# Attention and a squared-ReLU feed-forward on one core: the first product of the last 1024 tokens as seven block products, w_out's products in another order, attention's values two visits behind its scores

## The chip, the core and the metric

The kernel runs on one core of a Trainium2 chip. The metric is device time in microseconds. The time before is 602.68 us, the median of three runs (601.35 to 603.2).

## The reference, cut to what matters

Four sequences of 768 tokens with 8 heads of 64 go through a local attention with block summaries, and its output goes through a feed-forward of 512 -> 2048 -> 512:

```python
k_sum = k.reshape(B, H, nb, block, D).max(axis=3)        # block = 32
v_sum = v.reshape(B, H, nb, block, D).mean(axis=3)
scores_l = scale * q @ k.T, kept where abs(i - j) < 16
scores_s = scale * q @ k_sum.T + log(block)
a = softmax(concat(scores_l, scores_s))
attn = a @ concat(v, v_sum)
x = attn.transpose(0, 2, 1, 3).reshape(B * S, H * D)     # 3072 x 512
h = x @ w_in                                             # 512 x 2048
g = maximum(h, 0) ** 2
return g @ w_out                                         # 2048 x 512
```

## The kernel before, in words

Every operand of the feed-forward is split into a high and a low part (`xh`, `xl`; `gh`, `gl`; two parts of each weight tile), and each product is the sum of three (high x high, low x high, high x low). The 3072 tokens form six units of 512 tokens. A unit is eight groups of 64 tokens, and attention is done group by group, in visits of TensorE (`visit`, L809): one visit does the scores of two new groups (L597) and the products with the values of two older ones (L803), before at the distance of one visit. Between them lies a softmax on VectorE and ScalarE, a transpose of the probabilities on VectorE (L776, tile `a`), and a turn through DRAM: four stores to `turn` (L787) and one fetch (L793). The result of the values is split into `xh` and `xl` (L867, L870), a ring of 16 groups.

Units 0 and 1 (`ffn`, L955) are done plainly: for each of the 16 slices f of w_in, 12 matmuls of 128x512 give `h` (L979), ScalarE makes the ReLU and its square, and 12 matmuls with w_out's slice add up the output (L1003). In unit 0 the weights are also loaded and split.

The other 2048 tokens are two halves s = 0 and 1 of two units each. Their first product (`first_product`, L1183) is plain: 16 slices of 12 matmuls per unit (L1203). For their second product g is seen as 2 x 2 blocks (two slices f, two units), w_out likewise, and a scheme of seven block products replaces eight (`products`, L1238). A product j runs over the eight slice pairs p, with six matmuls of 128x512 for each p (L1316), so 56 steps of six for each s. Five operands of w_out's side are sums of blocks, made once by GpSimd (`combine`, L1062, with L1070 and L1085) and kept in DRAM; each step loads its 256 KB with a DMA (L1286) into a ring of eight places. On the side of g, three of the seven operands are sums of blocks made in place by VectorE (L1295), two more come out of the second unit's squares (L1232). For each step ScalarE makes the high part `gh` (L1300) and VectorE the low part `gl` (L1305); each of the two has three buffers. TensorE does four matmuls with `gh`, then two with `gl`. VectorE takes the finished products from PSUM (L1263).

The order on each engine is worked out before the program is recorded: every task has an engine, a cost, a key (when it is wanted) and the tasks and buffers that it needs, and a planner (`Plan.order`, L136) places them by key. On the chip each engine takes its instructions in that order, and waits by semaphores for the data alone. GpSimd also moves the block maxima of the keys (L610), which the next visit's scores need. All DMAs are issued from SyncE's queue.

Of the kernel before, what the change touches and what calls it, by code (L numbers as in the profile page):

```python
# [20 lines left out]
P = 128  # L21
# [15 lines left out]
NV = 3  # L37
# [12 lines left out]
FV_LEAD, FV1_LEAD = 2.0, 17.0  # L50
# [54 lines left out]

class Task:
# [6 lines left out]
class Plan:  # L113
# [13 lines left out]
    def add(self, name, engine, cost, emit, key, after=(), take=(), use=(), size=0, begin=0.0, behind=None, late=0.0):  # L127
        t = Task(name, engine, cost, emit, key, [a for a in after if a is not None], list(take), list(use), size, begin)
        t.behind, t.late = behind, late
        t.index = len(self.tasks)  # L130
        self.tasks.append(t)
        for b in t.take + t.use:
            b.users.append(t)
        return t

    def order(self):  # L136
# [29 lines left out]
        while events:  # L166
# [11 lines left out]
            for e, tasks in ready.items():  # L178
# [3 lines left out]
                t = next((t for t in tasks if t.begin <= now + 1e-9 and (t.behind is None or hasattr(t.behind, "start")) and can(t)), None)  # L182
# [23 lines left out]
def attention_then_relu2_ffn(  # L206
# [95 lines left out]
    FIRST_STEP = 3.2, 3.1, 2.8, 2.9  # L302
    PRODUCT_STEP = 1.55, 1.5, 1.4, 1.4
    A0, A1, B0, B1 = 12.0, 2.0, 21.0, 2.2
    HALF_AT = 25.0, 32.0
    SECOND = 0.0
    steps = [SLOW, STEP, *FIRST_STEP]
    unit_at, products_at, at = [], [], T0
    for u in range(NU):
        unit_at.append(at)  # L310
        at += NF * steps[u]
        if u >= PLAIN:
            products_at.append(at)
            at += (SOON, PRODUCTS - SOON)[(u - PLAIN) % 2] * NQ * PRODUCT_STEP[u - PLAIN]
    at_item = {(u, f): unit_at[u] + f * steps[u] for u, f in items}

    def wanted(g):
# [4 lines left out]
        lo, hi = unit_at[u - 1] + SECOND * (u == 1), unit_at[u] - LEAD * STEP  # L322
        if u >= NU - 2:
            ends = unit_at[NU - 3] - LEAD * STEP, unit_at[NU - 1] - LEAD * STEP
            mid = min(sum(ends) / 2, unit_at[NU - 2] - LEAD * STEP)
            lo, hi = (ends[0], mid) if u == NU - 2 else (mid, ends[1])
# [131 lines left out]
    def batch_v(b):  # L458
        key = wanted(b * NW - 1) - (FV_LEAD if b > 1 else FV1_LEAD) if b else -60
        out_ps = h_buf(f"vps{b}")  # L460
# [14 lines left out]
        for i in range(0, S // P, 2):  # L475
            if b == 1:
                x, xs = later_v[i], later_v[i : i + 2]
            elif b:
                x = buf("t", 3, (P, 2 * DM), F32, f"fv{b}_{i}")
# [4 lines left out]
            for k in range(2):  # L484
                new = not k and (b > 1 or i % 4 == 0)
# [3 lines left out]
                    key + (0.1 if b else 1) * (i + k) - 4 * (not b), behind=None if new else t, take=[x] * bool(new), use=[x] * (not new),  # L489
# [157 lines left out]
    def softmax(g, by_pe=False):  # L647
# [124 lines left out]
        else:  # L772


            def turn():
                nc.vector.transpose(  # L776
                    out=a.tile.rearrange("p (j n r) -> p j n r", j=NSQ, n=NPAIR),
# [4 lines left out]
            t_T[g] = add(f"T{g}", "DVE", 0.63, turn, due - 9, [t_n], take=[a], use=[pr])  # L782
            d = buf("turn", 4, (NSQ, SQ, NSQ, NPAIR * SQ), F32, f"turn{g}", dr)

            def store():
                for i in range(NSQ):
                    nc.sync.dma_start(  # L787
                        out=d.tile[:, :, i, :].rearrange("j c e -> c j e"),
                        in_=a.tile[i * SQ : (i + 1) * SQ].rearrange("c (j e) -> c j e", j=NSQ),
# [5 lines left out]
            t_w = add(f"TW{g}", "SP", 1.75, store, due - 8.5, [t_T[g]], take=[d], use=[a], size=4 * P * DM)  # L795
            t_A[g] = add(f"TR{g}", "SP", 0.35, fetch, due - 8, [t_w], use=[a, d], size=4 * P * DM)
# [11 lines left out]

    def visit(both, then=(), block_sums=None):  # L809

        n, g = len(both), both[-1]
        due = wanted(g)
        x_ps = h_buf(f"x{g}") if n == 2 else x_buf(f"x{g}")
# [9 lines left out]
        means_too = []  # L823
        take = [x_ps]
# [5 lines left out]
        if then:  # L830
# [4 lines left out]
            deps += keys_of(then[0], range(NPAIR)) + [t_QL[then[1]], window(then[1])] + [t_T[g] for g in both]  # L835
# [4 lines left out]
        def products():  # L840
# [8 lines left out]
            f"V{both[-1]}", "PE", 0.54 * n + 0.11 * (n == 1) + 0.49 * len(then) + 1.4 * bool(block_sums), products, due, deps,  # L849
            take=take + [s] * bool(s), use=use,  # L850
# [3 lines left out]
        for f in means_too:  # L854
            f()
        for g in then:
            t_S[g] = [t_v]
        cols = slice(both[0] % RING * TQ, (both[-1] % RING + 1) * TQ)
# [196 lines left out]
    scr_i = [dr.tile([P, 2 * DM], F32, name=f"scr_i{i}", tag=f"scr_i{i}") for i in range(NQ)]  # L1055


    ORDER = (0, 0), (0, 1), (1, 0), (1, 1), (1, 2), (0, 2), (1, 3)
# [3 lines left out]
    def combine(p):  # L1062

        due = unit_at[0] + 75 + 13.5 * p
        ws = [w_parts[1, 2 * p + k] for k in range(2)]
        raw = buf("t", 3, (P, 2 * DM), F32, f"cr{p}")
        sums = buf("t", 3, (P, 2 * DM), F32, f"cs{p}")
# [6 lines left out]
        def part(k, i):  # L1074
            return raw.tile[:, k * DM + i * HALF : k * DM + (i + 1) * HALF]
# [4 lines left out]
        def add_up():  # L1080
            for i, a, b, op in (
                (2, part(0, 1), part(1, 1), ALU.add), (0, of(2), part(0, 0), ALU.subtract),
                (1, part(0, 0), part(0, 1), ALU.subtract), (3, part(1, 0), of(0), ALU.subtract),
# [9 lines left out]
        def store():  # L1093
            for w, x in enumerate((raw, sums)):
                nc.sync.dma_start(
                    out=scr_s[p].rearrange("c p w x -> p c w x")[:, :, w], in_=x.tile.rearrange("p (c x) -> p c x", c=4)
                )
# [8 lines left out]
        for k in range(2):  # L1106
            t1.append(add(
                f"RC{p}_{k}", "POOL", 1.3, lambda k=k: whole(k), due + 1.3 * k, t_W[1, 2 * p + k],
                take=[raw, sums] * (not k), use=[raw] * k + ws[k], begin=due, behind=t1[0] if k else None,
            ))  # L1110
# [367 lines left out]
```

## Time and profile before

| | |
|---|---|
| median of three runs | 602.68 us |
| time of the profiled execution | 600.91 us |
| its span | 598.8 us |
| TensorE matmul busy | 581.8 us, 97% |
| VectorE busy | 394.1 us, 66% |
| ScalarE busy | 340.9 us, 57% |
| GpSimd busy | 67.3 us, 11% |
| granted TensorE clock | 0.999 |
| DMA traffic | 134.7 MB on the queue of the kernel |

PE is TensorE's matmuls, PEld its weight loads, DVE VectorE, ACT ScalarE, POOL GpSimd and SPq the queue of SyncE, from which DMAs are issued. In a row of a timeline stand the start, the duration, the engine, the line of the kernel, the operation, what it writes and reads, the size, how many, and in brackets how long the engine stood idle before it and who ended that. Lines are those of the kernel before.

### The profile page before, as it was taken

Reading aid. Unit: us, or ns where it says so; the run is one execution under the profiler, and the core shown is the slowest. Engines: PE = TensorE matmul, PEld = TensorE weight load, DVE = VectorE, ACT = ScalarE, POOL = GpSimd, SP = SyncE. Lnnn points to the kernel's source line nnn. Section 1 sums busy time; section 2 is a strip of 40 time slices with the busy share of each in tenths; the row PEclk is TensorE's granted clock in tenths of the full one; section 3 lists DMA queues with packets and bytes.
Section 4 is the critical chain, followed back from the end, with each engine's and each line's share of the span. In section 5 each row is a group of like instructions: output and inputs, shape, how many; then the busy total and the mean of one; then the engine's idle time right before and its main releaser. Section 6 shows DMA issues by size and latency. Waiting matters only on the chain.

```text
span 598.8 us, 11522 instructions
## 1 busy us (share of the span) xinstructions
PE 581.8 (97%) x4132; PEld 476.1 (80%) x4132; DVE 394.1 (66%) x692; ACT 340.9 (57%) x844; POOL 67.3 (11%) x117
## 2 busy tenths in 40 slices
PE   8889999979999999999999999999999999999996
PEld 6778888868888888888888787788888878888885
DVE  5999997767646815336855859897553643349763
ACT  2999885757736635446745656645453643455442
POOL 4300004333555200000000000000000000000000
PEclk9999999999999999999999999999999999999999
DMA  8999966859987885736856956889823762126772
GB/s 308 314 399 334 366 204 208 277 171 364 366 276 260 255 278 155 260 107 185 255 181 188 306 180 192 273 277 295 264 76 97 234 197 97 36 85 207 188 234 96
DMA packets 94428, 135.43 MB, mean 226 GB/s; under 512 B 9676, under 2 KB 50636, under 8 KB 94372
## 3 DMA queue, kind: packets, MB, share of 16 engines
q1 hardware_dynamic: 94372, 134.70, 69.6%
q8 instruction: 33, 0.54, 0.3%
q14 instruction: 23, 0.19, 0.1%
HBM read 98.22 MB, written 35.65 MB: 224 GB/s over the span
## 4 chain that ended last, share of the span: by engine, by line
PE 77%; DMA 8%; DVE 6%; ACT 6%; SPq 2%; issue 1%; DVEq 0%; ACTq 0%
PE h L1203 28%; PE o L1316 23%; PE o L1003 10%; PE h L979 9%; DMA raw<-wW 4%; PE x L803 3%; PE att L597 3%; ACT p L728 2%; DVE w L933 1%; DMA v<-vS 1%; DVE t L925 1%; DMA fv_lent<-vS 1%; DMA a<-turn 1%; DMA qvpa_lent<-qW 1%; ACT w L930 1%
## 5 line engine op out<-in xcount | busy, mean ns | idle before, releaser
L1203 PE MATMUL h<-xh,w 128*128 128x512 f32 x448 | 138.8, 391 | 0.5 <-ACT r L1213 0.5
L1316 PE MATMUL o<-gh,w 128*128 128x512 f32 x448 | 121.0, 391 | 0.4 <-ACT gh L1300 0.4
L1300 ACT CAST gh<-g 128x512 fp32r<-128x512 f32 x112 | 68.9, 620 | 53.3 <-DVE gl L1305 25.8
L1203 PEld LDWEIGHTS h<-xh,w 128*128 128x128 f32 x448 | 83.6, 188 | 18.7 <-ACT r L1213 1.3
L1316 PEld LDWEIGHTS o<-gh,w 128*128 128x128 f32 x448 | 83.5, 188 | 18.4 <-ACT gh L1300 0.9
L1305 DVE TENSOR_TENSOR gl<-g,gh 128x512 fp32r<-128x512 f32 x112 | 76.0, 687 | 28.4 <-ACT gh L1300 28.3
L1203 PE MATMUL h<-xl,w 128*128 128x512 f32 x224 | 87.2, 389 | 0.0
L1213 ACT ACTIVATE r<-h 128x512 f32<-128x512 f32 x64 | 38.0, 596 | 86.3 <-PE h L1203 73.0
L979 PE MATMUL h<-xh,w 128*128 128x512 f32 x240 | 74.1, 390 | 0.0
L728 ACT ACTIVATE p<-p,nm 128x118 f32<-128x118 f32 x160 | 61.1, 388 | 16.6 <-DVE nm L692 16.6
L1316 PE MATMUL o<-gl,w 128*128 128x512 f32 x224 | 69.4, 390 | 1.1 <-DVE gl L1305 1.1
L1003 PE MATMUL o<-w,gh 128*128 128x512 f32 x240 | 61.6, 393 | 1.9 <-ACT gh L990 1.9
L1003 PEld LDWEIGHTS o<-w,gh 128*128 128x128 f32 x240 | 44.5, 188 | 11.7 <-ACT gh L990 2.3
L979 PEld LDWEIGHTS h<-xh,w 128*128 128x128 f32 x240 | 44.9, 188 | 9.4
L1316 PEld LDWEIGHTS o<-gl,w 128*128 128x128 f32 x224 | 41.9, 188 | 10.6 <-DVE gl L1305 2.0
L1203 PEld LDWEIGHTS h<-xl,w 128*128 128x128 f32 x224 | 42.0, 188 | 8.8
L979 PE MATMUL h<-xl,w 128*128 128x512 f32 x120 | 46.7, 389 | 0.0
L993 DVE TENSOR_TENSOR gl<-r,gh 128x512 fp32r<-128x512 f32 x30 | 22.6, 755 | 34.9 <-ACT gh L990 30.6
L610 POOL COPY kb<-kb 128x96 f32<-128x96 f32 x25 | 9.5, 382 | 289.3 <-ACT kw L622 120.2
L676 DVE SCALAR_TENSOR_TENSOR p<-att,mask 128x236 f32<-128x236 f32 x76 | 26.5, 395 | 16.5 <-PE att L597 16.3
L988 ACT ACTIVATE r<-h 128x512 f32<-128x512 f32 x30 | 17.8, 592 | 32.2 <-PE h L979 32.2
L1003 PE MATMUL o<-w,gl 128*128 128x512 f32 x120 | 33.7, 390 | 1.3 <-DVE gl L993 1.3
(147 smaller groups left out, 841.6 us busy)
## 6 DMA issues: line engine op xcount, KB each, us to landing
raw<-wW SPq DMA_DIRECT2D x32, 512.0 KB, 7.2
w<-scr_s SPq DMA_DIRECT2D x64, 256.0 KB, 3.2
w<-scr_a SPq DMA_DIRECT2D x48, 256.0 KB, 3.6
turn<-a SPq DMA_DIRECT2D x160, 64.0 KB, 2.2
a<-turn SPq DMA_DIRECT2D x40, 256.0 KB, 4.5
w<-scr_i SPq DMA_DIRECT2D x40, 256.0 KB, 3.4
v<-vS SPq DMA_DIRECT2D x33, 192.0 KB, 3.2
kb<-kT SPq DMA_DIRECT2D x16, 384.0 KB
```

Source lines behind the costliest of these rows:

```text
L597: nc.tensor.matmul(score_at(g, part, j)[c * TQ : (c + 1) * TQ, :], lhsT=q_bufs[g].tile[rows, p, :] if term else unscale[rows, :], rhs=(mas ...
L676: nc.vector.scalar_tensor_tensor(out=pr.tile[:, j, :KEYS], in0=x, scalar=SCALE, in1=mask_of(g)[0].unsqueeze(1).broadcast_to([P, x.shape[1] ...
L728: nc.scalar.activation(x, score_tile(g, p % parts)[:, p] if by_pe else x, AF.Exp, bias=nm.tile[:, p : p + 1], scale=SCALE if by_pe else 1. ...
L803: nc.tensor.matmul(x_of(i)[h % 2 * D : (h % 2 + 1) * D, h // 2, :], lhsT=v_bufs[g].tile[:KEYS, h * D : (h + 1) * D], rhs=av[:KEYS, 2 * c : ...
L979: nc.tensor.matmul(cut(h), lhsT=lhs.tile[:, k * P : (k + 1) * P], rhs=rhs[:, k, c0 : c0 + n], start=(i == 0), stop=(i == 3 * KT - 1),)
L993: lambda: nc.vector.tensor_tensor(out=cut(gl), in0=cut(r), in1=cut(gh).bitcast(F32), op=ALU.subtract),
L1003: nc.tensor.matmul(o_of(o, t), lhsT=terms[i][0].tile[:, (t - t0) * P : (t - t0 + 1) * P], rhs=terms[i][1].tile, start=(first and i == 0), ...
L1203: nc.tensor.matmul(h.tile, lhsT=lhs.tile[:, k * P : (k + 1) * P], rhs=rhs[:, k, c0 : c0 + TU], start=(i == 0), stop=(i == 3 * KT - 1),)
L1213: t2 = add(f"RL{name}", "ACT", 0.56, lambda: nc.scalar.activation(r.tile, h.tile, AF.Relu), due + 3, [t1], take=[r], use=[h])
L1300: f"GH{s}_{n}", "ACT", 0.54, lambda x=x, gh=gh: nc.scalar.copy(out=gh.tile, in_=x.tile), due - 4, ready,
L1305: lambda x=x, gh=gh, gl=gl: nc.vector.tensor_tensor(out=gl.tile, in0=x.tile, in1=gh.tile.bitcast(F32), op=ALU.subtract),
L1316: nc.tensor.matmul(o.tile[:, d], lhsT=chunk.tile[:, w * HALF + d * P : w * HALF + (d + 1) * P], rhs=y.tile, start=begins and w == 0 and y ...
```

## The change

It has three parts, and many numbers of the planner are set anew beside them.

First product of the last 1024 tokens. The plain first products of units 4 and 5 go. In their place `x` is seen as 2 x 2 blocks (two halves of its 512 columns, two units), w_in as 2 x 2 blocks (two halves of its rows, two slices f), and a new function `sweep` makes seven block products for each slice pair p, 56 steps of six matmuls. Four sums of blocks of `x` are made by VectorE and split again (`sum_x`). Four sums of blocks of w_in are made by GpSimd (`combine(0, p)`, in the time of units 2 and 3) and kept in DRAM; all of w_in is now kept there too (`keep`). Product 6 of a pair adds to the bank of product 5 once VectorE has read that. With the first product in blocks, the squares of g come from PSUM by way of VectorE's additions. All of the second product of the last half then follows in one piece.

Second product. The order of the seven products is another (`ORDER`); the three sums of blocks of g, for products 3, 5 and 6 (`SUMS_POOL`), are made by GpSimd and no longer by VectorE, as is one of the sums that came out of the second unit's squares (line of `SD`). U1 and P5 are copied by ScalarE.

Attention. The values of a pair of groups are done two visits behind its scores and no longer one; the transposed probabilities have a buffer of their own (`st`), and the fetched ones take a place of `a` only when they are fetched. The buffers of values are two and no longer three. One visit holds scores alone, two hold values alone. Block sums of values are loaded into three places taken at once.

```diff
-NV = 3
+NV = 2
...
-    ORDER = (0, 0), (0, 1), (1, 0), (1, 1), (1, 2), (0, 2), (1, 3)
+    ORDER = (0, 0), (0, 1), (1, 2), (1, 0), (1, 3), (1, 1), (0, 2)
+    SUMS_POOL = 3, 5, 6
...
+            st = buf("st", 1, (P, DM), F32, f"st{g}")
...
-            t_T[g] = add(f"T{g}", "DVE", 0.63, turn, due - 9, [t_n], take=[a], use=[pr])
+            t_T[g] = add(f"T{g}", "DVE", 0.63, turn, due - 9, [t_n], take=[st], use=[pr])
...
-            t_w = add(f"TW{g}", "SP", 1.75, store, due - 8.5, [t_T[g]], take=[d], use=[a], size=4 * P * DM)
-            t_A[g] = add(f"TR{g}", "SP", 0.35, fetch, due - 8, [t_w], use=[a, d], size=4 * P * DM)
+            t_w = add(f"TW{g}", "SP", 1.75, store, due - 8.5, [t_T[g]], take=[d], use=[st], size=4 * P * DM)
+            t_A[g] = add(f"TR{g}", "SP", 0.35, fetch, due - 8, [t_w], take=[a], use=[d], size=4 * P * DM)
...
         t3 = add(f"SQ{name}", "ACT", 0.54, lambda: nc.scalar.activation(r.tile, r.tile, AF.Square), due + 4, [t2], use=[r])
-        other, to = (even[s, p], last) if odd else (first, diff)
-        even[s, p] = r
-        t_G[s, p, 2 + odd] = add(
-            f"SD{name}", "DVE", 0.62, lambda: nc.vector.tensor_tensor(out=to.tile, in0=r.tile, in1=other.tile, op=ALU.subtract),
-            due + 5, [t3, t_G[s, p, 0]], use=[r, other, to],
+        t_G[s, p, 2] = add(
+            f"SD{name}", "POOL", 1.45, lambda: nc.gpsimd.tensor_tensor(out=diff.tile, in0=r.tile, in1=first.tile, op=ALU.subtract),
+            due + 5, [t3, t_G[s, p, 0]], use=[r, first, diff],
         )
...
                 x, ins, op = (
-                    (first, None, None), (second, None, None), (first, (last, first), ALU.add), (last, None, None),
-                    (diff, None, None), (second, (second, first), ALU.subtract), (diff, (first, diff), ALU.add),
+                    (first, None, None), (second, None, None), (diff, None, None), (diff, (last, diff), ALU.subtract),
+                    (last, None, None), (first, (diff, first), ALU.subtract), (second, (second, diff), ALU.subtract),
                 )[j]
...
                 if op is not None:
+                    on_pool = j in SUMS_POOL
+                    engine = nc.gpsimd if on_pool else nc.vector
                     ready = [add(
-                        f"TA{s}_{n}", "DVE", 0.62,
-                        lambda x=x, ins=ins, op=op: nc.vector.tensor_tensor(out=x.tile, in0=ins[0].tile, in1=ins[1].tile, op=op),
-                        due - 5, ready, use=[x, *ins],
+                        f"TA{s}_{n}", "POOL" if on_pool else "DVE", 1.45 if on_pool else 0.62,
+                        lambda x=x, ins=ins, op=op, engine=engine: engine.tensor_tensor(
+                            out=x.tile, in0=ins[0].tile, in1=ins[1].tile, op=op
+                        ),
+                        due - 6, ready, use=[x, *ins],
                     )]
...
+    def sweep():
...
+        def product(p, j, o, begins, deps):
...
+            def mm():
+                hi, lo = operand[j]()
+                todo = [(k, w, y) for w, y in ((0, hi), (1, hi), (0, lo)) for k in range(2)]
+                for i, (k, w, y) in enumerate(todo):
+                    nc.tensor.matmul(
+                        o.tile, lhsT=chunk.tile[:, w * HALF + k * P : w * HALF + (k + 1) * P], rhs=y[:, k],
+                        start=begins and i == 0, stop=i == 5, skip_group_check=not begins,
+                    )
...
+        one(0)
+        for p in range(NQ):
+            if p + 1 < NQ:
+                one(p + 1)
+            two(p)
...
+        for p in range(NQ):
...
+            t, due = product(p, 3, b, True, [])
+            t_u2 = plus(f"Q2_{p}", u2, b, last, due + 2, [t, kept[p]], [u2])
+            t5, _ = product(p, 2, e, True, [])
+            t, due = product(p, 5, b, False, [t_u2])
+            t_u3 = plus(f"Q3_{p}", u3, b, last, due + 2, [t], [u3])
+            t_c22 = plus(f"Q22_{p}", u3, e, u3, due + 2.8, [t_u3, t5])
+            if p:
+                last_one(p - 1)
+            t, due = product(p, 6, b, False, [t_u3])
+            t_c21 = plus(f"Q21_{p}", second, b, last, due + 2, [t])
...
-                visit([g - 2, g - 1], [g, g + 1], sums)
+                lag = 2 if g <= FIRST_S else 4
+                visit([] if g == FIRST_S + 2 else [g - lag, g - lag + 1], [g, g + 1], sums)
```

How the instructions stand on the engines is shown at two places. A row has the line, the operation, what is written and read, and the size; `x4` is the number of equal ones. `gh` and `gl` are the high and the low part of an operand of g with the number of the step, `g_0` to `g_7` are the eight places of one set of g's blocks.

The first place is the second product of the last 1024 tokens, steps 33 to 39 of its 56. On VectorE before, sums of g (L1295) and low parts (L1305) alternate:

```order
L1295 TENSOR_TENSOR g_1_4896<-g_1_4896 128x512
L1305 TENSOR_TENSOR gl_35_5968<-g_3_5032,gh_35_5964 128x512
L1295 TENSOR_TENSOR g_2_4950<-g_2_4950 128x512
L1305 TENSOR_TENSOR gl_36_5980<-g_4_5076,gh_36_5976 128x512
L1295 TENSOR_TENSOR g_3_5032<-g_3_5032 128x512
L1305 TENSOR_TENSOR gl_37_5992<-g_5_5110,gh_37_5988 128x512
L1295 TENSOR_TENSOR g_4_5076<-g_4_5076 128x512
L1305 TENSOR_TENSOR gl_38_6004<-g_6_5196,gh_38_6000 128x512
L1295 TENSOR_TENSOR g_5_5110<-g_5_5110 128x512
L1295 TENSOR_TENSOR g_6_5196<-g_6_5196 128x512
L1305 TENSOR_TENSOR gl_39_6023<-g_7_5259,gh_39_6012 128x512
```

On VectorE now, at steps 32 to 38, the low parts (now L1371) stand alone but for one addition of a finished product (now L1317):

```order
L1371 TENSOR_TENSOR gl_32_6087<-g_0_5171,gh_32_6083 128x512
L1371 TENSOR_TENSOR gl_33_6099<-g_1_5181,gh_33_6095 128x512
L1317 TENSOR_TENSOR u_1_6110<-o_67,u_1_5823 128x1024
L1371 TENSOR_TENSOR gl_34_6119<-g_2_5204,gh_34_6107 128x512
L1371 TENSOR_TENSOR gl_35_6125<-g_3_5224,gh_35_6121 128x512
L1371 TENSOR_TENSOR gl_36_6136<-g_4_5248,gh_36_6133 128x512
L1371 TENSOR_TENSOR gl_37_6148<-g_5_5268,gh_37_6145 128x512
L1371 TENSOR_TENSOR gl_38_6160<-g_6_5290,gh_38_6157 128x512
```

The sums now stand on GpSimd (now L1358), 24 of them in a row with nothing between; the last five of one product and the first four of the next:

```order
L1358 TENSOR_TENSOR g_3_5224<-g_3_5224 128x512
L1358 TENSOR_TENSOR g_4_5248<-g_4_5248 128x512
L1358 TENSOR_TENSOR g_5_5268<-g_5_5268 128x512
L1358 TENSOR_TENSOR g_6_5290<-g_6_5290 128x512
L1358 TENSOR_TENSOR g_7_5311<-g_7_5311 128x512
L1358 TENSOR_TENSOR g_0_5171<-g_0_5171 128x512
L1358 TENSOR_TENSOR g_1_5181<-g_1_5181 128x512
L1358 TENSOR_TENSOR g_2_5204<-g_2_5204 128x512
L1358 TENSOR_TENSOR g_3_5224<-g_3_5224 128x512
```

What moved: the 24 sums of 128x512, from the queue of the engine that makes the low parts to another engine's queue, in which they come one straight behind the other. Before, GpSimd has only copies of block maxima (L610) in this part of the program.

The second place is TensorE in the first product of the last 1024 tokens. Before, each of its 32 items is twelve matmuls into one bank of `h`:

```order
L1203 MATMUL h_11_5652<-xh,w_849 128x512 x2
L1203 MATMUL h_11_5652<-xl,w_849 128x512
L1203 MATMUL h_11_5652<-xh,w_849 128x512 x2
L1203 MATMUL h_11_5652<-xl,w_849 128x512
L1203 MATMUL h_11_5652<-xh,w_849 128x512 x2
L1203 MATMUL h_11_5652<-xl,w_849 128x512
L1203 MATMUL h_11_5652<-xh,w_849 128x512 x2
L1203 MATMUL h_11_5652<-xl,w_849 128x512
```

Now the seven products of a pair stand there by sixes (now L1536), into banks `sb`, `att` and `o`; `xs` and some `w` places hold sums of blocks of x; the first rows are of pair 0, the last two begin pair 1:

```order
L1536 MATMUL sb_0_5322<-w_948,w_1022 128x512 x4
L1536 MATMUL sb_0_5322<-xs_5246,w_1022 128x512 x2
L1536 MATMUL att_68<-w_916,w_1022 128x512 x4
L1536 MATMUL att_68<-xs_5215,w_1022 128x512 x2
L1536 MATMUL sb_0_5322<-w_1022,w_1027 128x512 x4
L1536 MATMUL sb_0_5322<-xs_5236,w_1027 128x512 x2
L1536 MATMUL sb_0_5322<-w_1027 128x512 x4
L1536 MATMUL sb_0_5322<-w_862,w_1027 128x512 x2
L1536 MATMUL sb_1_5358<-w_948,w_916 128x512 x4
L1536 MATMUL sb_1_5358<-xs_5246,w_916 128x512 x2
```

What moved: a pair's products 3, 5 and 6 add up in one bank of `sb`, and each of the later two must wait until VectorE has read the one before. Between products 3 and 5 stands product 2 (`att_68`); between products 5 and 6 of pair 0 stands nothing, and in the later pairs the last product of the pair before.

More of the change, by code (lines that the diff above doesn't have):

```diff
@@ L1356, in attention_then_relu2_ffn @@
+    att_slots = Slots(None, "atts", 2, [att[i].rearrange("p a b -> p (a b)") for i in range(2)])
     batch_k(0)
@@ L1393, in attention_then_relu2_ffn @@
     done = []
-    for u in range(NU):
-        groups(min((u + 1) * UG + 2, NG))
+    for u in range(PLAIN + 2):
+        groups(min((u + 1) * UG + 4, NG))
         if u >= PLAIN:
@@ L1412, in attention_then_relu2_ffn @@
             ffn(u, f, o, done)
+    groups(NG)
+    sum_x()
+    products(1, range(PRODUCTS), products_at[2], PRODUCT_STEP[2], sweep())
     for t in plan.tasks:
```

420 lines of the change are left out of this document (318 added, 102 removed).

## The prediction

> **What bounds the kernel now.** I read the totals of the page first, then the chain that ended last, then the groups by line, the busy time by stage, and last the timeline of the stages that the change touches. The totals and the chain:
>
> ```profile
> span 598.8 us, 11522 instructions
> PE 581.8 (97%) x4132; PEld 476.1 (80%) x4132; DVE 394.1 (66%) x692; ACT 340.9 (57%) x844; POOL 67.3 (11%) x117
> PE 77%; DMA 8%; DVE 6%; ACT 6%; SPq 2%; issue 1%; DVEq 0%; ACTq 0%
> 496.22 43.52 PE h L1203 x192
> 539.74 54.41 PE o L1316 x240
> ```
>
> TensorE is busy 97% of the span, and from 496 us to 594 us the chain is nothing but its matmuls. One matmul of 128x512 takes 43.52 / 192 = 0.2267 us there, and 54.41 / 240 gives the same. So a step of six takes 1.36 us, and whatever leaves TensorE's queue is gained unless another engine then comes too late. Which one could is read by stage (columns: window, length, busy PE, PEld, DVE, ACT, POOL with counts, clock, DMA share, GB/s):
>
> ```profile
> 350.00:408.00 58.00, 56.45 (x450) 45.43 (x449) 52.70 (x100) 35.18 (x98) 1.07 (x4) 1.00 0.78 245
> 540.00:594.00 54.00, 54.00 (x239) 44.48 (x237) 39.26 (x59) 24.30 (x39) 0.00 (x0) 1.00 0.64 185
> PE o L1316 <- DVE gl L1305: 1.1, 2, 0.6
> ```
>
> In the products of the first half (350 to 408 us) VectorE is 91% busy, and TensorE's waits there are for `gl`. In those of the last half VectorE has a quarter of its time free. GpSimd does next to nothing in either.
>
> **Removed: 48 matmuls.** The plain first product of units 4 and 5 is 32 items of twelve, 384 matmuls; the block products are 56 steps of six, 336. 48 x 0.2267 = 10.9 us leave TensorE's queue, all in the stretch where the chain is TensorE alone. The second product keeps its 56 steps per half.
>
> **Moved: 24 block sums per half from VectorE to GpSimd.** They cost VectorE this:
>
> ```profile
> L1295 DVE TENSOR_TENSOR g<-g 128x512 f32<-128x512 f32 x48 | 32.4, 687 | 0.5
> 189.23 2.55 POOL L1070 TENSOR_TENSOR cr<-w 128x512 f32<-128x512 f32 x2
> 190.66 1.67 DVE L993 TENSOR_TENSOR gl<-r,gh 128x512 fp32r<-128x512 f32 x1 [3.38 <-ACT gh L990]
> 186.00 0.73 POOL L1085 TENSOR_TENSOR cs<-cr 128x256 f32<-128x256 f32 x1 [4.18 <-DMA scr_s<-cr]
> 186.11 1.16 DVE L993 TENSOR_TENSOR gl<-r,gh 128x512 fp32r<-128x512 f32 x1
> 186.81 1.06 POOL L1085 TENSOR_TENSOR cs<-cs,cr 128x256 f32<-128x256 f32 x1
> 187.83 0.74 POOL L1085 TENSOR_TENSOR cs<-cr 128x256 f32<-128x256 f32 x1
> ```
>
> VectorE is relieved of 24 x 0.687 = 16.5 us per half. But the other rows show that the two engines do not add from SBUF at the same time. GpSimd's second sum runs from about 190.5 to 189.23 + 2.55 = 191.78; VectorE's `gl` begins inside it and ends at 190.66 + 1.67 = 192.33, so it did its work only in the last 0.55. It lasted 1.67 where one takes 0.687: 0.98 of waiting. At 186 us they take turns: GpSimd until 186.73, `gl` until 186.11 + 1.16 = 187.27, GpSimd until 187.87. The 128x256 sum that lasts 0.74 alone ended 0.60 behind `gl`, so 0.14 of it went on beside `gl`. If each sum of 128x512 (2.55 / 2 = 1.27 alone) is followed by one `gl`, a turn takes 1.27 - 0.14 + 0.54 = 1.68 us. A step of TensorE takes 1.36. That is why the sums, free in GpSimd's own time, can set TensorE's pace: every step needs a `gl`, and in the last half the 24 sums follow each other without a gap in GpSimd's queue.
>
> How late may `gl` come? In the last half:
>
> ```profile
> 554.94 0.69 DVE L1305 TENSOR_TENSOR gl<-g,gh 128x512 fp32r<-128x512 f32 x1 [0.67 <-ACT gh L1300]
> 558.16 0.61 PE L1316 MATMUL o<-gl,w 128*128 128x512 f32 x2
> ```
>
> With three buffers of `gl`, the one finished at 555.63 is read at 558.16: 2.5 us of slack. Last half: 24 x (1.68 - 1.36) = 7.7, less 2.5, is **+5.2 us**. Its bounds: 0, if GpSimd's sums fall behind and VectorE gets two `gl` between them; 24 x 0.6 - 2.5 = 11.9, if nothing overlaps (1.27 + 0.69 = 1.96 per turn). I take the turn that the rows show.
>
> The Trainium skill, "SBUF — State Buffer", section "Who interferes with whom", says that VectorE and GpSimd share one pair of ports as an exclusive lock held for the whole instruction, and that a VectorE instruction with two SBUF inputs contends with a GpSimd read. By that rule to the letter the turn is 1.96 and the last half costs 11.9, an estimate which would put the whole sum at +4.3 where I come to -2.4; the trace agrees that the loser stands still, but shows 0.14 of overlap and 0.54 for the `gl` behind it.
>
> In the first half the sums stand among visits of attention:
>
> ```profile
> L1316 PE MATMUL o<-gh,w 128*128 128x512 f32 x112 | 30.5, 394 | 0.4 <-ACT gh L1300 0.4
> L1316 PE MATMUL o<-gl,w 128*128 128x512 f32 x56 | 17.5, 394 | 1.1 <-DVE gl L1305 1.1
> L1203 PE MATMUL h<-xh,w 128*128 128x512 f32 x28 | 8.6, 389 | 0.0
> L1203 PE MATMUL h<-xl,w 128*128 128x512 f32 x14 | 5.4, 389 | 0.0
> ```
>
> In these 58 us stand 112 + 56 + 28 + 14 = 210 matmuls of 128x512, 47.6 us; less 1.5 of waiting, 8.9 are left for six visits, about 1.5 each. The changed stage has 40 steps (54.4 us) and three visits (4.5), 58.9 us or 1.47 per step. The same turn of 1.68 then costs 24 x 0.21 = 5.0, less 2.5 of slack: **+2.5 us**. It holds only if VectorE's other work fits beside GpSimd's sums. What reads one operand from PSUM or only reduces does: `p<-att,mask`, `nm`, the transposes. Lower bound 0; the upper bound is a rival below.
>
> **Added: the sweep.** Products 3, 5 and 6 of a pair add up in one bank, with VectorE's reading between. Between products 3 and 5 stands product 2, 1.36 us, which covers the reading:
>
> ```profile
> 594.17 1.29 DVE L1263 TENSOR_TENSOR u<-o,u 128x512 f32<-128x512 f32 x2 [3.18 <-PE o L1316]
> ```
>
> 1.29 / 2 = 0.65 us. Between products 5 and 6 of pair 0 nothing stands, so that reading is in the open: **+0.8 us** with the signals there and back. In pairs 1 to 7 the preceding pair's last product covers it; without that cover they would cost 7 x 0.8 = 5.6, the upper bound.
>
> **Moved: fetches and visits.** The values come two visits later, so that the fetch has more time; but in the changed order the shortest stretch between two visits is 30 matmuls of 128x512, 6.8 us, where before it was 60.
>
> ```profile
> a<-turn SPq DMA_DIRECT2D x40, 256.0 KB, 4.5
> v<-vS SPq DMA_DIRECT2D x33, 192.0 KB, 3.2
> w<-scr_a SPq DMA_DIRECT2D x48, 256.0 KB, 3.6
> ```
>
> 4.5 us still fit in 6.8, but SyncE's queue now holds more: the step loads of the sweep, and the eight more stores of w_in. I take 0, since the second visit of distance is the cover; without it a visit would stand for up to 5 us. One visit more than before stands alone among the wide matmuls: **+0.4 us**, an estimate of a quarter of a visit's 1.5, between 0 and 1.5. GpSimd's eight new `combine` (2 x 1.27 + 4 x 0.74 = 5.5 us each) run in units 2 and 3 where it was idle; they are inside the second term's uncertainty. The copies moved to ScalarE cost nothing: it is 24.30 of 54 us busy.
>
> **The sum** against the profiled execution, 600.91 us (its span is 598.8): -10.9 + 5.2 + 2.5 + 0.8 + 0.4 = -2.0, so 598.9. The median of the runs shown is 1.8 above that execution: **600.7 us**.
>
> **Rivals.**
>
> *No turn-taking on the path.* The `gl` slack, and sums that slip behind two `gl`, absorb the lock. For it: the sums have 40 steps of time (54 us) for 24 x 1.27 = 30 us. Against: they follow without gaps, and the trace shows strict turns wherever the two meet. -10.9 + 1.2 = -9.7: 591.2, or 593.0 as a median. Chance 0.25.
>
> *VectorE becomes the bound in the first half.* There it is 91% busy, and its instructions in the stage only fall from 115 to 107, since other work moves in for the 24 sums; at 0.527 each (52.70 / 100) that is 4 us less. Each sum of GpSimd holds up one addition of VectorE, by between 0.47 (1.16 - 0.69) and 0.98, in the mean 0.73: 24 x 0.73 = 17.5 us of new standing against 5.3 us free (58.00 - 52.70) and the 4 gained, so 8.2 us on the path in place of 2.5. It decides from 9.3 us of standing, 0.39 per sum. Then -2.0 + 5.7 = +3.7, and with the last half at the 11.9 of turns without overlap +10.4: 606.4 to 613.1, middle about 609. For it: TensorE's waits there are for `gl` already. Against: half of VectorE's work there does not touch the lock. Chance 0.27.
>
> *Fetches or the sweep stall too.* All upper bounds of these two (5 and 5.6, in place of 0 and 0.8) on the forecast: 610.5; on the rival before, about 619. Chance 0.1.
>
> That the change does not do what it says is left out: the instructions of the new kernel hold the 48 matmuls fewer and the 48 sums on GpSimd.
>
> **How the numbers follow.** The forecast has a chance of 0.38, with a range of its own of 597 to 605. Faster or slower by 0.3% is what a measurement of this kernel can tell, so the bounds are 600.9 and 604.5. Faster: the first rival, and 0.23 of the forecast's 0.38: 0.48. Same: 0.1 of the forecast's, and 0.01. Slower: 0.05 of the forecast's, the second and the third rival, less the 0.01: 0.41. The range of 592 to 615 leaves out the lower part of the first rival and the upper part of the third.
>
> **What would show it.** Right: in the last half of the new profile sums on GpSimd with means near 1.7 us instead of 1.27, `gl` with a mean near 1.2 instead of 0.69, and TensorE waiting for `gl` by about 5 us there; one wait of under 1 us in pair 0 of the sweep and no other. Wrong: GpSimd's sums near 1.27 or TensorE without waits beside them (then 593), or waits of `x` for `a<-turn`, or VectorE without idle time in the first half (then 606 and more).

## The result and the profile after

The changed kernel takes 624.94 us (median of 4 runs, 621.97 to 630.25) against 602.45 for the kernel before: a ratio of 1.038, 95% interval 1.031 to 1.046. It is slower by 22.5 us where 2.0 us less was forecast, and outside the range of 592 to 615.

The page of the changed kernel, totals and two groups (line, engine, operation, names, shape, count; busy us, mean ns; idle before):

```profile
span 622.0 us, 11742 instructions
PE 587.5 (94%) x4084; PEld 467.4 (75%) x4084; DVE 454.0 (73%) x680; ACT 354.2 (57%) x866; POOL 214.6 (35%) x221
L1358 POOL TENSOR_TENSOR g<-g 128x512 f32<-128x512 f32 x48 | 79.8, 1695 | 139.7 <-DVE gl L1371 139.7
L1371 DVE TENSOR_TENSOR gl<-g,gh 128x512 fp32r<-128x512 f32 x112 | 111.1, 1019 | 19.8 <-ACT gh L1366 15.0
```

VectorE has 12 instructions fewer and 60 us more of busy time. The low parts `gl` last 1.02 us in the mean instead of 0.687, and a sum on GpSimd 1.70 instead of 1.27: both contain standing.

What TensorE waited for (total us, times, longest), and the three stages of the changed kernel: products of the first half, sweep with the last visits, products of the last half (window, length, busy PE, PEld, DVE, ACT, POOL, clock, DMA share, GB/s):

```profile
PE o L1382 <- DVE gl L1371: 9.8, 7, 3.5
PE o L1382 <- DMA w<-scr_a: 2.3, 1, 2.3
PE o L1536 <- ACT g L1567: 2.1, 2, 1.3
PE o L1536 <- ACT g L1559: 1.8, 3, 0.7
```

```profile
367.30:449.90 82.60, 69.71 (x465) 50.57 (x463) 76.91 (x100) 39.45 (x108) 49.24 (x33) 0.98 0.75 245
449.90:534.80 84.90, 79.68 (x370) 63.79 (x370) 45.58 (x60) 42.75 (x75) 0.00 (x0) 1.00 0.62 189
534.80:617.00 82.20, 81.45 (x337) 61.44 (x335) 65.73 (x62) 37.31 (x61) 39.90 (x24) 1.00 0.61 179
```

A busy PE here is not a PE at its step: in the last row it is busy 81.45 of 82.20 us with 336 matmuls that need 76.2. So the loss is read from lengths. Last half: 82.2 - 76.2 = 6.0 us. Sweep: 336 matmuls again, 76.2, and 1.8 of visits: 6.9. First half: 240 matmuls are 54.4 us and its narrow matmuls 8.5 (from their starts in the timeline, with 1.0 us of waiting for a fetch among them), so 19.7 are lost; in the kernel before the stage from 356.5 to 426.6 lost 3.3 in the same reckoning (70.1 less 252 x 0.2267 and 9.6 of narrow ones), which leaves 16.4. With one wait of 2.3 for a step load at 303 us, and the 10.9 us of removed matmuls, that makes -10.9 + 6.0 + 6.9 + 16.4 + 2.3 = +20.7 of the 22.9 us by which TensorE's last matmul is later (616.9 against 594.0). Another 1.7 us stand behind that wait at 303 us: from 300 to 310 us the granted clock was 0.83, and 10 x 0.17 = 1.7. That brings the sum to 22.4.

The last half, in the timeline of the changed kernel:

```profile
572.47 6.84 POOL L1358 TENSOR_TENSOR g<-g 128x512 f32<-128x512 f32 x4
572.98 6.88 DVE L1371 TENSOR_TENSOR gl<-g,gh 128x512 fp32r<-128x512 f32 x4
575.38 1.09 PE L1382 MATMUL o<-gh,w 128*128 128x512 f32 x4
...
576.51 0.30 PEld L1382 LDWEIGHTS o<-gl,w 128*128 128x128 f32 x2 [0.47 <-DVE gl L1371]
...
577.08 1.09 PE L1382 MATMUL o<-gh,w 128*128 128x512 f32 x4
```

Four sums in 6.84 us, four `gl` in 6.88, and TensorE's step from 575.38 to 577.08: all three go at 1.70 us. The first half looks otherwise:

```profile
388.05 8.57 POOL L1358 TENSOR_TENSOR g<-g 128x512 f32<-128x512 f32 x5
...
390.26 1.26 DVE L767 TENSOR_SCALAR nm<-nm 128x4 f32<-128x4 f32 x1
391.55 0.18 DVE L768 RECIPROCAL nm<-nm 128x4 f32<-128x4 f32 x1
391.65 2.16 DVE L1450 TENSOR_TENSOR xt<-xh,xl 128x1024 f32<-128x1024 f32 x1
393.73 1.75 DVE L1371 TENSOR_TENSOR gl<-g,gh 128x512 fp32r<-128x512 f32 x1
...
395.53 0.75 PE L1382 MATMUL o<-gl,w 128*128 128x512 f32 x2 [3.47 <-DVE gl L1371]
396.11 1.89 PE L1382 MATMUL o<-gh,w 128*128 128x512 f32 x4
397.85 1.23 PE L1382 MATMUL o<-gl,w 128*128 128x512 f32 x2
```

Here three VectorE instructions, one soon after the other, stand behind GpSimd's sums before the `gl` that TensorE needs is done: one on 4 columns for 1.26 us, the first sum of x for 2.16, `gl` itself for 1.75. TensorE waits 3.47 us. Behind that wait its four matmuls take 397.85 - 396.11 = 1.74 us instead of 0.91.

### The profile page after: what moved, and what is told of

Read it like the earlier page. It is cut to its first block, busy times and chain, and to the rows that moved or that the text cites. A ratio compares the mean times of both kernels' runs of the same rounds, so it can differ in the third digit from the quotient of the medians.

```text
span 622.0 us, 11742 instructions
## 1 busy us (share of the span) xinstructions
PE 587.5 (94%) x4084; PEld 467.4 (75%) x4084; DVE 454.0 (73%) x680; ACT 354.2 (57%) x866; POOL 214.6 (35%) x221
## 4 chain that ended last, share of the span: by engine, by line
PE 70%; DMA 12%; DVE 9%; issue 4%; ACT 3%; SPq 1%; DVEq 0%; ACTq 0%
PE o L1037 14%; PE o L1382 13%; PE h L1013 12%; PE h L1255 12%; PE sb L1536 5%; DVE gl L1371 5%; PE att L1536 3%; PE o L1536 3%; PE x L832 3%; PE att L624 2%; DMA kb<-kT 2%; DMA a<-turn 2%; DMA w<-scr_a 1%; DMA qvpa_lent<-vF 1%; DMA scr_t<-cri 1%
## 5 line engine op out<-in xcount | busy, mean ns | idle before, releaser
L1358 POOL TENSOR_TENSOR g<-g 128x512 f32<-128x512 f32 x48 | 79.8, 1695 | 139.7 <-DVE gl L1371 139.7
L1371 DVE TENSOR_TENSOR gl<-g,gh 128x512 fp32r<-128x512 f32 x112 | 111.1, 1019 | 19.8 <-ACT gh L1366 15.0
L1382 PE MATMUL o<-gl,w 128*128 128x512 f32 x224 | 74.4, 413 | 12.6 <-DVE gl L1371 9.8
L1013 PE MATMUL h<-xh,w 128*128 128x512 f32 x240 | 74.4, 391 | 0.0
L1255 PE MATMUL h<-xh,w 128*128 128x512 f32 x224 | 69.5, 391 | 0.0
L1013 PEld LDWEIGHTS h<-xh,w 128*128 128x128 f32 x240 | 44.7, 188 | 9.4
L1255 PEld LDWEIGHTS h<-xh,w 128*128 128x128 f32 x224 | 41.7, 188 | 8.8
L1013 PE MATMUL h<-xl,w 128*128 128x512 f32 x120 | 46.7, 389 | 0.0
L1027 DVE TENSOR_TENSOR gl<-r,gh 128x512 fp32r<-128x512 f32 x30 | 28.0, 933 | 22.3 <-ACT gh L1024 19.4
L1255 PE MATMUL h<-xl,w 128*128 128x512 f32 x112 | 43.6, 389 | 0.0
L1117 POOL TENSOR_TENSOR cro<-w 128x512 f32<-128x512 f32 x16 | 25.2, 1598 | 43.6 <-PE vps L525 26.4
L1265 ACT ACTIVATE r<-h 128x512 f32<-128x512 f32 x32 | 19.1, 596 | 34.0 <-PE h L1255 32.4
L805 DVE STREAM_TRANSPOSE st<-p 128x512 f32<-128x512 f32 x40 | 28.3, 706 | 13.1 <-DMA turn<-st 12.9
L1022 ACT ACTIVATE r<-h 128x512 f32<-128x512 f32 x30 | 17.8, 593 | 29.2 <-PE h L1013 29.2
```

Of the source, the lines that this page charges most:

```text
L805: nc.vector.transpose(out=st.tile.rearrange("p (j n r) -> p j n r", j=NSQ, n=NPAIR), in_=pr.tile.rearrange("p n (j c) -> p j n c", c=SQ),)
L1013: nc.tensor.matmul(cut(h), lhsT=lhs.tile[:, k * P : (k + 1) * P], rhs=rhs[:, k, c0 : c0 + n], start=(i == 0), stop=(i == 3 * KT - 1),)
L1027: lambda: nc.vector.tensor_tensor(out=cut(gl), in0=cut(r), in1=cut(gh).bitcast(F32), op=ALU.subtract),
L1117: nc.gpsimd.tensor_tensor(out=raw.tile[:, k * DM : (k + 1) * DM], in0=ws[k][0].tile.bitcast(F32), in1=ws[k][1].tile.bitcast(F32), op=ALU.add)
L1255: nc.tensor.matmul(h.tile, lhsT=lhs.tile[:, k * P : (k + 1) * P], rhs=rhs[:, k, c0 : c0 + TU], start=(i == 0), stop=(i == 3 * KT - 1),)
L1358: lambda x=x, ins=ins, op=op, engine=engine: engine.tensor_tensor(out=x.tile, in0=ins[0].tile, in1=ins[1].tile, op=op),
```

## The experiments

The theory is that of the turns: a sum on GpSimd and an addition on VectorE from SBUF do not run together. Its rivals: the first half's loss comes from too much work on VectorE, of attention or other; and late loads or ScalarE's high parts.

**All sums back on VectorE**, everything else as changed:

```diff
-    SUMS_POOL = 3, 5, 6
+    SUMS_POOL = ()
```

> The changed kernel with all 48 block sums back on VectorE; the rest as changed. Turns of GpSimd and VectorE as the cause of the last half's loss: its 56 steps, which took 82 us in the changed kernel, take 76.5, and TensorE's step stays at 1.36 there. In the first half the turns say that 24 sums of 0.69 (16.5 us) come onto VectorE and about 15 us of its waiting go, so the stage stays about as long as now (82 us for 240 matmuls and its visits): 619 in all. If the first half's loss were the turns alone and VectorE had room, that stage would fall to about 66 and the total to 604. If GpSimd's sums had cost nothing there, the total would grow by 10 or more.

It took 606.40 us, ratio to the kernel before 1.007 (1.005 to 1.010). Its three stages:

```profile
364.80:438.30 73.50, 66.09 (x465) 50.37 (x463) 71.83 (x125) 39.91 (x108) 9.51 (x9) 1.00 0.86 278
438.30:521.50 83.20, 79.14 (x370) 63.75 (x370) 45.48 (x60) 43.04 (x75) 0.00 (x0) 1.00 0.64 190
521.50:597.60 76.10, 76.10 (x337) 62.85 (x335) 57.24 (x86) 37.38 (x61) 0.00 (x0) 1.00 0.66 193
```

The last half is back at TensorE's pace, 76.1. The first half gained 9.1 us where I expected nothing, and the total is 606.40 where I expected 619: with 25 instructions more, VectorE is busy 5 us less. So the sums on GpSimd cost VectorE more in standing (5 + 16.5, about 21 us) than the 16.5 us that they saved it. Still 73.5 us is 7.3 more than 54.4 + 8.5 + 3.3: moving the sums explains 18.5 of the 22.5 us, and the rest of the change is no gain either.

**Only the last half's sums back on VectorE**:

```diff
-                    on_pool = j in SUMS_POOL
+                    on_pool = j in SUMS_POOL and s == 0
```

> The changed kernel with only the last half's 24 sums back on VectorE. Turns: the last half falls from 82 to 76.5 us, nothing else moves, 619.5 in all. If the last half's slow steps have another cause (late chunks, ScalarE's high parts), the steps of 1.70 us stay and the total stays at 625.

619.87 us (1.029, 1.023 to 1.034): 5.1 less than the changed kernel. Its last half:

```profile
538.50:614.60 76.10, 76.10 (x337) 62.86 (x335) 57.27 (x86) 37.41 (x61) 0.00 (x0) 1.00 0.65 193
```

From 82.2 to 76.1, as the turns have it.

**The kernel before, with sums on GpSimd**: first the last half's alone, then all.

```diff
+                    on_pool = s == 1
+                    engine = nc.gpsimd if on_pool else nc.vector
...
-                        f"TA{s}_{n}", "DVE", 0.62,
-                        lambda ...: nc.vector.tensor_tensor(...),
-                        due - 5, ready, use=[x, *ins],
+                        f"TA{s}_{n}", "POOL" if on_pool else "DVE", 1.45 if on_pool else 0.62,
+                        lambda ...: engine.tensor_tensor(...),
+                        due - (6 if on_pool else 5), ready, use=[x, *ins],
```

In the second, `on_pool = True`. The three dots in a line mark arguments left out here.

> The kernel before with the last half's 24 sums moved to GpSimd and nothing else. Turns: 24 sums of about 1.70 us in place of 1.27, TensorE's step 1.70 beside them, and 24 x 0.34 = 8.2 us less the 2.5 of gl's slack: +5.7, 608. If a sum on GpSimd costs the path nothing by itself: 602.5, the same.

> The kernel before with all 48 sums on GpSimd: its first half too, where attention is spread over a longer stretch than in the changed kernel. If the turns by themselves cost the first half some 10 us: 614. If they cost that only because the changed kernel squeezes attention into the 40 steps of the products: the first half grows by at most 2.5, and with the 2 of the last half 606 or less.

The first took 604.12 us (1.003, 1.000 to 1.005), the second 608.81 (1.014, 1.010 to 1.018). The products of the kernel before in its first half, and 2 to 6 of its last half:

```profile
356.50:426.60 70.10, 68.55 (x557) 55.29 (x557) 62.05 (x118) 42.16 (x121) 1.34 (x5) 1.00 0.82 260
539.60:594.00 54.40, 54.40 (x241) 44.84 (x239) 39.66 (x59) 24.30 (x39) 0.00 (x0) 1.00 0.64 185
```

The same stages of the same kernel with all sums on GpSimd:

```profile
356.70:432.80 76.10, 71.74 (x557) 57.53 (x556) 65.17 (x102) 42.25 (x121) 25.81 (x21) 0.96 0.79 239
544.80:602.10 57.30, 56.91 (x241) 44.06 (x239) 45.72 (x45) 24.12 (x39) 26.06 (x16) 1.00 0.60 177
```

In the last half the sums cost 2.9 us and not the 5.7 that I expected. Eight of the 24 begin ahead of this stage, beside the plain first product, where no `gl` is made; six of these stand alone and take 1.29 us each. For the others 16 x 0.34 = 5.4 less the slack of 2.5 is 2.9, a reckoning made afterwards. In the first half they cost 6.0, between the 2.5 of the turns and the 10 that I gave: VectorE loses 16 instructions in that window and gains 3.1 us of busy time. TensorE stands 2.8 us more there (76.1 - 71.74 against 70.1 - 68.55), which is near the turns' 2.5; the other 3.2 are matmuls that last longer, at a granted clock of 0.96. Of this kernel's 24 sums of the first half, 16 fall into the stage, so a sum costs 6.0 / 16 = 0.38 us. In the changed kernel all 24 fall into it, and 9.1 / 24 is 0.38 too: these runs do not show that the changed kernel makes the single sum dearer, it has more of them in the stage.

**Every sum as two instructions of half the size**, on GpSimd as in the changed kernel:

```diff
+                    def add_up(x=x, ins=ins, op=op, engine=engine, pieces=2 if on_pool else 1):
+                        for k in range(pieces):
+                            c = slice(k * TU // pieces, (k + 1) * TU // pieces)
+                            engine.tensor_tensor(out=x.tile[:, c], in0=ins[0].tile[:, c], in1=ins[1].tile[:, c], op=op)
...
-                        lambda x=x, ins=ins, op=op, engine=engine: engine.tensor_tensor(
-                            out=x.tile, in0=ins[0].tile, in1=ins[1].tile, op=op
-                        ),
...
```

> The changed kernel with every one of the 48 sums still on GpSimd, but as two instructions of 128x256 instead of one of 128x512: the same elements, a shorter stay each. Turns held for a whole instruction: a turn is then 0.60 + 0.54 = 1.14 us, less than TensorE's step of 1.36, so that the last half goes at 1.36 per step (76.5 us in place of 82), and in the first half VectorE stands half as long each time: its stage from 82.6 to some 77, 614 in all. If what matters is how many elements GpSimd moves beside VectorE, not how long one instruction holds: 625, the last half still at 82.

613.77 us (1.021, 1.015 to 1.028). Its four runs lie in two pairs, at 610 and at 617 to 618 us, so the total is known less well than in the other experiments; the profiled run took 610.52. First and last half, the group of the sums, and a piece of the last half's timeline:

```profile
364.40:441.10 76.70, 67.64 (x465) 49.75 (x464) 70.74 (x100) 38.93 (x108) 57.61 (x57) 1.00 0.83 263
527.10:603.50 76.40, 76.40 (x337) 62.80 (x335) 55.56 (x62) 37.40 (x61) 49.85 (x48) 1.00 0.65 193
```

```profile
L1359 POOL TENSOR_TENSOR g<-g 128x256 f32<-128x256 f32 x96 | 98.9, 1068 | 126.0 <-DVE gl L1372 126.0
```

```profile
562.92 0.69 DVE L1372 TENSOR_TENSOR gl<-g,gh 128x512 fp32r<-128x512 f32 x1 [0.52 <-ACT gh L1367]
564.28 1.18 DVE L1372 TENSOR_TENSOR gl<-g,gh 128x512 fp32r<-128x512 f32 x1 [0.67 <-ACT gh L1367]
565.64 0.96 DVE L1372 TENSOR_TENSOR gl<-g,gh 128x512 fp32r<-128x512 f32 x1 [0.18 <-ACT gh L1367]
```

GpSimd moves as many elements and is busy longer (98.9 us against 79.8), and yet the last half is back at 76.4 and the first is down to 76.7, as expected. What counts is how long one instruction keeps the other engine out. With 0.60 + 0.54 per turn VectorE is ahead of TensorE's 1.36 again, and waits for `gh` between its `gl`. The same work on the same engines is 5.9 and 5.8 us shorter in the two stages, by the length of one instruction.

**The start of the sweep.** Its products 0 and 1 of a pair add up in one bank, with a copy by ScalarE between, and one other product in that time:

```diff
         one(0)
+        one(1)
         for p in range(NQ):
-            if p + 1 < NQ:
-                one(p + 1)
+            if p + 2 < NQ:
+                one(p + 2)
             two(p)
```

> The changed kernel with the first products of a pair two pairs ahead of the second ones in the first 16 steps of the sweep (they add up in one bank, with ScalarE's copy between; one other product stands between them now, two then). If that copy is what TensorE waits for there (gaps of 0.4 to 1.3 us between 455 and 478, some 4 us): 4 us less, 621. If the sweep's start is held by ScalarE's total work, or by loads: the same, 625.

619.90 us (1.030, 1.025 to 1.035), 5.0 less than the changed kernel, of which its sweep shows 3.1: 81.8 against 84.9. TensorE's waits for ScalarE there fell from 3.9 to 1.1 us.

```profile
449.20:531.00 81.80, 79.04 (x369) 63.85 (x369) 45.34 (x60) 42.65 (x75) 0.00 (x0) 1.00 0.65 197
```

**Both edits together** (all sums on VectorE, and the lead of two pairs), and then, on top of them, the first two sums of x out of the first half's last steps (the diff is shortened; the call also gets `begin=sweep_at`):

```diff
-        do("R1", 0, ..., ALU.add, due - 15, of_unit[0] + [sums[0][-1]["C12"]])
-        do("R4", 3, ..., ALU.add, due - 14, of_unit[0])
+        do("R1", 0, ..., ALU.add, due + 0.5, of_unit[0] + [sums[0][-1]["C12"], t_G[0, NQ - 1, "in", 6]])
+        do("R4", 3, ..., ALU.add, due + 1, of_unit[0] + [t_G[0, NQ - 1, "in", 6]])
```

> The changed kernel with all sums on VectorE and the first products of a pair two pairs ahead in the sweep: the two gains together, 606.4 - 4 = 602.4, the same as before the change. If the second gain hid behind the first: 606.

> As the kernel before this one (all sums on VectorE, two pairs ahead), and the first two block sums of x on VectorE (1.2 us each) come behind the last low part of the first half rather than among its last steps. If VectorE's work is what the end of the first half waits for (1.2 us gaps for gl from 426 to 435 us): 2.4 us less, 600. If those waits have another cause: the same as without it.

605.98 us (1.007, 1.004 to 1.011) and 603.44 (1.003, 1.001 to 1.005). The two edits do not add up: with the sums on VectorE the lead of two pairs brought nothing that shows (605.98 against 606.40), where 4 us were expected: TensorE's waits for ScalarE in the sweep had come down to 2.0 us with the sums on VectorE alone, and are 1.5 with both. The late sums of x brought 2.5 us where 2.4 were expected. But they came ahead of VectorE's last addition from the bank that the sweep begins in:

```profile
439.55 1.40 PE L1536 MATMUL o<-xh,w 128*128 128x512 f32 x4 [2.14 <-DVE u L1317]
440.75 1.05 PE L1536 MATMUL o<-xl,w 128*128 128x512 f32 x2
441.60 1.91 PE L1536 MATMUL o<-xh,w 128*128 128x512 f32 x4
```

So I put them behind it (their last condition is then `sums[0][-1]["C21"]`):

> As the kernel with late sums of x, but these two come behind the last addition of a finished product (1.2 us on VectorE), for whose bank the sweep's first matmul waits. If that order is what held the sweep's start (a gap of 2.1 us, and some 4 us of matmuls at half speed behind it): 3 us less than the kernel with late sums of x, 600.5. If the bank isn't what it waits for: the same, 603.4.

604.00 us (1.003, 1.000 to 1.007), where 600.5 was expected: a miss. The wait at the sweep's first matmul fell from 2.14 to 1.32 us and its matmuls ran at full speed, but the total did not follow. What took the 2 us back isn't settled.

**Less work on VectorE**: in the kernel of the last run, the division of the probabilities left out, or given to ScalarE, for the last 8 groups. The first of the two does not compute the reference.

```diff
         def normal():
+            if g >= 40:
+                return
```

```diff
+        def one_of(p):
+            x = pr.tile[:, p, :KEYS]
+            nc.scalar.activation(x, x, AF.Copy, scale=nm.tile[:, 2 * NPAIR + p : 2 * NPAIR + p + 1])
```

> As e10, and the division of the probabilities by their sum (VectorE, 0.65 us with two SBUF inputs) is left out for the last 8 groups, so that their output is another; all other instructions stay in their order. If VectorE's total work bounds the products of the first half (98% busy in each slice of it): 8 x 0.65 = 5.2 us of work less, most of it in that stage, 4 us less than e10. If the bound there is the chain of attention (scores, softmax, turn, fetch) or TensorE: the same as e10.

> As e10, and that division is done by ScalarE for the last 8 groups (four instructions of 128x118 each, some 0.3 us apiece by its other ones of that size, so 10 us more on ScalarE, which is some 65% busy in that stage). If VectorE's work is the bound: 3 to 4 us less than e10, near or under the time before the change. If ScalarE's high parts of g then come late: as e10 or slower.

600.22 us (0.998, 0.995 to 1.001) and 604.73 (1.004, 1.001 to 1.006). Left out, the 5.2 us of work gave 3.8 in all. The products of the first half without and with the division (the second is the kernel with the sums of x behind the addition):

```profile
363.70:431.00 67.30, 64.57 (x465) 50.39 (x463) 65.22 (x115) 40.30 (x108) 9.14 (x9) 1.00 0.95 303
```

```profile
367.70:439.00 71.30, 66.04 (x465) 50.40 (x463) 69.64 (x123) 39.77 (x107) 9.54 (x9) 1.00 0.89 289
```

Eight instructions and 4.4 us less on VectorE, 4.0 us less in length: VectorE, busy 97 to 98% of that stage in both, is its bound even with none of the 24 sums of g on GpSimd. The division also stands in the chain of attention, but that is not what TensorE waited for: in the stage with the division its waits are 4.5 us for `gl` and 0.3 us for the fetched probabilities. Given to ScalarE, the same work gave nothing, a miss. TensorE's waits in this run (total us, times, longest):

```profile
PE x L841 <- DMA a<-turn: 4.1, 3, 2.4
...
PE o L1391 <- DVE gl L1380: 1.7, 3, 1.0
```

The waits for `gl` fell from 4.5 us to 1.7, and those of the values for their fetch rose from 2.1 to 4.1: the chain of attention came next. No version that computes the reference was faster than the kernel before; the nearest stand at 603 to 606.

## Why the prediction was wrong

- The 48 matmuls went as forecast, 10.9 us, and the last half's term was right in mechanism and size: +5.2 forecast, +6.0 measured, by turns of 1.70 us where 1.68 was worked out; undone alone it gave 5.1 back. The whole sum under turns without overlap was given as +4.3 against -2.4, which leaves out the 0.4 us of the visit: with it the two are +4.7 and -2.0.
- **The step that failed is the first half's +2.5**, of which I wrote that it holds only if VectorE's other work fits beside GpSimd's sums. It did not: the stage lost 16.4 us more than before. I priced the turn against TensorE's step, as if `gl` were all that VectorE does from SBUF. The division (1.16 us in the mean instead of 0.64), the sums of x (1.69 instead of 1.21 with the sums on VectorE), the low parts of w_in's sums (1.66 instead of 1.38) and even the 128x4 operation on `nm` (0.63 instead of 0.15) take turns too, several of them in a row ahead of one `gl`. The transposes (0.70), `p<-att,mask` (0.39) and the reduction into `nm` (0.62) kept their time, as I wrote. The rival in which VectorE becomes the bound had the right mechanism, and its 8.2 was half of the price. It reckoned 17.5 us of standing against 9.3 us of free time. By the kernel with the sums on VectorE, VectorE's other work in the stage is 71.83 - 15.8 = 56.0 us, so that the standing was 76.91 - 56.0 = 20.9; TensorE's own work there is 54.4 + 8.5 = 62.9, so that 6.9 were free; and VectorE idles for another 5.7 of the 82.6 us. 20.9 - 6.9 + 5.7 are the 19.7 lost, 16.4 more than before.
- Taking the sums off GpSimd gave 9.1 of the 16.4 back. The other 7.3 are VectorE's work itself: with the sums on VectorE it is busy 71.83 of 73.5 us. It is not attention that grew: the stage has eight divisions of the probabilities in both kernels. In the new order the third product of a half needs no sum, so all three sets of sums fall into the stage, while the kernel before makes one set of eight ahead of it; and two sums of x and two low parts of w_in's sums come on top. The stage in the kernel before, and in the changed kernel with the sums on VectorE:

```profile
L1295 DVE TENSOR_TENSOR g<-g 128x512 f32<-128x512 f32 x16 | 10.7, 686 | 0.0
L747 DVE TENSOR_TENSOR p<-p,nm 128x472 f32<-128x472 f32 x8 | 5.2, 644 | 0.2
...
L1358 DVE TENSOR_TENSOR g<-g 128x512 f32<-128x512 f32 x23 | 15.8, 694 | 0.0
L774 DVE TENSOR_TENSOR p<-p,nm 128x472 f32<-128x472 f32 x8 | 6.0, 756 | 0.0
L1140 DVE TENSOR_TENSOR csi<-csi,cri 128x1024 fp32r<-128x1024 f32 x2 | 2.8, 1375 | 0.0
L1450 DVE TENSOR_TENSOR xt<-xh,xl 128x1024 f32<-128x1024 f32 x2 | 2.4, 1214 | 0.0
```

  That this work is the bound is shown in part, by the 4.0 us that leaving out the division took from the stage.
- The sum has no term for the clock. Behind the wait of 3.47 us in the first half and behind that for the step load at 303 us TensorE's matmuls ran at half speed for a while: the granted clock was 0.79 from 394 to 402 us and 0.83 from 300 to 310, 1.7 us each.
- The sweep: the wait between products 5 and 6 of pair 0 came as priced, 0.8 us forecast, 0.78 here:

```profile
466.12 1.20 PE L1536 MATMUL o<-xh,w 128*128 128x512 f32 x4 [1.28 <-ACT g L1567]
...
484.28 1.20 PE L1536 MATMUL sb<-w 128*128 128x512 f32 x4 [0.78 <-DVE u L1582]
```

  But I looked at that bank alone. Products 0 and 1 of a pair have the same kind of chain through ScalarE, with one product between them, and waited 3.9 us in the first 16 steps; the sweep lost 6.9 in all.
- The loads and fetches, taken at 0: two step loads of 2.3 and 1.6 us (the second inside the first half's 16.4) and 1.6 us for the fetch of the probabilities (0.9 in the kernel before), 5.5 in all where 5 was the bound. Setting the values back to one visit behind was not tried; what that part of the change costs or brings by itself stays open.
- The slower cases had 0.41 of the chance and the right mechanisms, and were priced too low: the measured time lies 10 us beyond the range, by the first half's standing, the sweep's chain and the step load.

## What to carry to other kernels

Before work is moved to an engine that is idle, ask what the two engines share, and price it by the instruction that stands behind the longest stay of the other, not by elements: here the kernel with the same sums in halves took 11 us less. Price it against all that the waiting engine does in that stage, not against the one operation that the path needs. And when an order is changed, count again what each engine has to do in each stage: here eight more sums of g and two sums of x fell into a stage in which VectorE had had 8 us free.

## What the runs showed of the hardware

An operation on 4 columns does not escape the turns. The `nm` of the first half took 1.26 us beside GpSimd's sums (the rows at 388.05 and 390.26 above); with GpSimd idle it takes 0.15, in the kernel with late sums of x:

```profile
431.33 0.15 DVE L767 TENSOR_SCALAR nm<-nm 128x4 f32<-128x4 f32 x1
```

The Trainium skill, "SBUF — State Buffer", section "Who interferes with whom", names tensor_scalar among the operations that can take the port pair shared with GpSimd, and says that the loser stands for the whole instruction. The traces agree, and the run with half-sized sums shows what follows from it: the size of the other engine's instruction is the price.

A wait of TensorE can cost again behind it. After 3.47 us of standing its next matmuls took 0.43 us each in place of 0.227 (the rows from 395.53), and after 2.14 us those at 441.60 took (443.31 - 441.60) / 4 = 0.43 too. The granted clock was 0.92 from 438 to 460 us in that kernel:

```profile
438.00:460.00 22.00, 19.70 (x104) 15.40 (x104) 12.76 (x12) 11.73 (x19) 0.00 (x0) 0.92 0.59 185
```

That is 22 x 0.08 = 1.8 us lost, about as much as the 1.7 of each of the two places in the changed kernel. The length of the wait alone does not decide. In the kernel before with all sums on GpSimd, four matmuls behind a wait of 1.89 us took (373.11 - 371.49) / 4 = 0.41 us each, and the granted clock was 0.79 from 370 to 378 us. In the changed kernel with the last half's sums on VectorE, a wait of 2.20 us ended at 156.24 us, and the clock from 156 to 162 us was 1.00. Behind the wait of 1.32 us at 440 us, in the kernel with the sums of x behind the addition, the clock stayed at 1.00 too.

The Trainium skill, "TensorE: Matmul & The Clock Gate", section "Part 1: The HAM clock gate (the "warmup" mystery)", says that the array falls to half its clock after an idle window of about 3.4 us and comes back after a busy one. The half clock agrees, and 1.7 us lost at half clock are 3.4 us of it; but here waits of 1.89 and 2.14 us were enough, and one of 2.20 us was not.
